# Attention with two mixtures of experts: weights converted from their upper 16 bits, engines chosen by the list, and the list's order kept on every compute engine in the first part

## The chip, the cores and the metric

The kernel runs on one core of one Trainium2 chip. The metric is the device time of one execution in microseconds (us). The kernel before has a median of 1095.64 us over 3 runs (1090.09 to 1098.15).

## The reference

Three blocks follow each other. Chunked attention works on q, k and v of 8 batches, 8 heads, 576 positions and 64 dimensions; every chunk of 64 positions attends to itself alone. Its output x has 4608 rows of 512. The second block is a feed-forward layer with a squared ReLU, and the third a soft mixture of 8 experts with 4 slots each:

```python
scores = scale * np.matmul(q_c, k_c.transpose(0, 1, 2, 4, 3))
attn = softmax(scores); out = np.matmul(attn, v_c)     # chunks of 64
h = np.maximum(x @ w_in, 0.0)                          # 512 -> 2048
x = h * h @ w_out                                      # 2048 -> 512
logits = x @ phi                                       # 32 slots
slot_input = softmax(logits, 0).T @ x
slot_out[e] = np.maximum(slot_input[e] @ w1[e], 0.0) @ w2[e]
out = softmax(logits, 1) @ slot_out
```

w_in and w_out lie in memory as 8-byte numbers (float64). [...]

## The kernel before, in words

The 4608 rows are cut into 36 tiles of 128, and the tiles into blocks: block 0 has one tile, block 1 two, blocks 2 to 12 three each. The hidden width 2048 is cut into 16 columns f of 128. A step (b, f) is the work of block b on column f. On TensorE (PE) it is `moe_h`, 12 matmuls (line 702), then, when the other engines have finished, `moe_out`, three matmuls per tile (lines 753, 754, 755). Between the two stand four elementwise instructions: relu (718 on ScalarE, ACT; 720 on VectorE, DVE), sq (725 or 727), gh (152, 157 or 161, the helper `copy`) and gl (737). gh and gl are the high and low part of the squared number, wi and wo the high and low parts of the weights.

A column of weights must be converted before its first step. `conv(f)` has two halves, a = 0 for w_in and a = 1 for w_out. `load` fetches 512 KB into a staging buffer, shifted by one byte, so that a number's top byte can be read as an int8 and 32 of the bits below it as an int32. `kept` (239 or 241, DVE) clips the top byte, `number` (246 ACT, 248 DVE or 250 GpSimd, POOL) copies it, `rest` (259 POOL, 254 DVE) subtracts the two, `lead` (line 154, ACT) scales the difference into the leading bits of a float, and `join` (265, DVE) shifts the int32 right by 5 and ors the leading bits in. Then `total`, `reduce` and `finish` (146, 169, 177 to 182) find a power-of-two scale of w_in, `hi` and `lo` (154 or 159, and 309) make wi, `whi` and `wlo` (152 or 157, and 319) make wo. There are four sets of staging buffers, and some sets are homes of later wo columns.

The attention of a tile i is a chain of its own. Tiles 0 to 6 run in 4-byte floats (`attention32`): transposes (576), copies to qbd and qkT, scores (593), max, less, exp, sums, normal (619), transposes (626), values (637), xh and xl (645, 650). Later tiles run in pairs of 2-byte parts (`attention`).

The first part of the program holds all 16 conversions, tiles 0 to 8 and the steps of blocks 0, 1, 2 and 13 (block 13 is a second pass over tiles 0 to 2 for the columns that blocks 0 and 1 left out). `list_schedule` orders it: each operation has a cost, an engine, what it depends on and a rank (`RANK_T`, `RANK_F`, `RANK_S`); the list takes, engine by engine, the operation that can start first, and among those that start within `AHEAD` (1.17 us) the one of lowest rank. The engine of an operation comes from tables written out by hand (`ON_U`, `ON_HI`, `ON_GL` and others). The phases of steps are set by `PARTS` = (7, 12): blocks 0 and 1 on f = 0 to 6, block 2 on f = 0 to 11, block 13 on f = 7 to 15, block 2 on f = 12 to 15. The list's order is binding on SyncE (SP), which issues the loads, alone (`IN_ORDER`); on the compute engines the framework's own scheduler places the instructions.

After the first part come blocks 3 to 12 with 16 steps each, in the order in which the code is written, and a tail with the experts.

Of the kernel before, what the change touches and what calls it, by code (L numbers as in the profile page):

```python
# [22 lines left out]
TOP = 2.0 ** 27  # L23
PARTS = (7, 12)
IN_ORDER = ('SP',)
AHEAD = 1.1702665353509787
ON_U = {(0, 0): 'act', (0, 1): 'act', (1, 0): 'act', (1, 1): 'pool', (2, 0): 'act', (2, 1): 'act', (3, 0): 'act', (3, 1): 'act', (4, 0): 'both', (4, 1): 'act', (5, 0): 'act', (5, 1): 'pool', (6, 0): 'act', (6, 1): 'act', (7, 0): 'act', (7, 1): 'act', (8, 0): 'dve', (8, 1): 'act', (9, 0): 'pool', (9, 1): 'act', (10, 0): 'act', (10, 1): 'pool', (11, 0): 'pool', (11, 1): 'pool', (12, 0): 'act', (12, 1): 'act', (13, 0): 'act', (13, 1): 'both', (14, 0): 'act', (14, 1): 'dve', (15, 0): 'act', (15, 1): 'dve'}
ON_PHI = {1: 1, 8: 1, 2: 1, 5: 1, 6: 0, 4: 1, 3: 1}
ON_WLO = {2: 0, 1: 1, 9: 0, 6: 1, 14: 1, 13: 0, 15: 0, 8: 1, 7: 1}
ON_SQ = {(0, 2): 'pool', (0, 1): 'pool', (0, 0): 'act', (13, 3): 'dve', (13, 2): 'dve', (2, 1): 'act', (2, 3): 'act', (1, 0): 'dve', (13, 0): 'pool', (0, 3): 'dve', (1, 2): 'dve'}  # L30
RANK_T = [-6.3129014593893205, 8.385327230567464, 13.762703571034038, 15.13222949110116, 41.022113092835795, 44.95494613298783, 56.80756465669842, 83.16639749144919, 93.32411425998357]
RANK_F = [-22.66145244618513, 22.55189538058041, 33.54199552023938, 45.42389033691279, 51.173403669572345, 53.0591736226747, 66.09437067068046, 77.9705914776398, 75.74661162051322, 94.18996216021172, 99.04476119923027, 98.70569850048518, 116.04666246008468, 115.83019197755651, 117.2519817658151, 162.90219728291348]
RANK_S = 13.647708445823483
# [5 lines left out]
ON_Q = {(6, 2): 'dve', (8, 1): 'act', (8, 3): 'dve', (4, 0): 'dve', (7, 0): 'act', (3, 0): 'dve', (0, 1): 'act', (2, 2): 'act', (4, 1): 'dve', (1, 1): 'dve', (7, 2): 'act', (1, 2): 'act', (4, 2): 'act', (4, 3): 'act', (3, 3): 'act', (0, 0): 'dve', (1, 0): 'dve', (6, 3): 'act', (6, 1): 'act'}  # L39
ON_V = {(5, 0): 'act', (2, 0): 'pool', (1, 1): 'dve', (7, 1): 'pool', (0, 1): 'act', (2, 1): 'pool', (6, 1): 'act', (3, 0): 'dve', (1, 0): 'act', (8, 1): 'act', (8, 0): 'dve'}  # L40
ON_N = {6: 'dve', 8: 'dve', 5: 'pool', 3: 'pool', 7: 'dve', 1: 'pool', 0: 'pool'}
ON_HI = {6: 'dve', 7: 'dve', 10: 'act', 15: 'dve', 8: 'act', 13: 'pool'}
ON_LEAD = {}
ON_WHI = {5: 'act', 9: 'dve', 3: 'dve', 14: 'dve', 6: 'act', 11: 'dve', 2: 'act', 15: 'dve', 7: 'act'}
ON_RELU = {(13, 3): 'dve', (1, 3): 'dve', (13, 0): 'act', (13, 1): 'act', (0, 0): 'dve', (1, 2): 'act', (2, 3): 'act', (0, 3): 'dve', (13, 2): 'act'}
ON_GH = {(1, 2): 'pool', (13, 3): 'dve', (13, 1): 'pool', (0, 0): 'act', (13, 0): 'act', (2, 3): 'dve', (13, 2): 'pool', (1, 0): 'act', (0, 3): 'pool', (1, 3): 'pool', (2, 1): 'act'}
ON_GL = {(13, 3): 'dve', (13, 0): 'dve', (2, 1): 'dve', (1, 2): 'dve', (0, 2): 'dve', (0, 1): 'pool'}


class Op:  # L50


    def __init__(self, eng, cost, deps, stage, fn):
        self.eng, self.cost, self.deps, self.stage, self.fn = eng, cost, deps, stage, fn
# [3 lines left out]
def kernel(  # L58
# [46 lines left out]
    ones = const.tile([P, P], BF16, name="ones")  # L105
    phi_sb = const.tile([P, KT, NS], F32, name="phi_sb")
# [88 lines left out]
    def conv(f):  # L195
# [40 lines left out]
        def kept(a):  # L236
            on_u = ON_U.get((f, a), "act")
            if on_u == "both":
                dve.tensor_scalar(half(a, 1), byte(a), 56.0, None, ALU.max)
            else:  # L240
                dve.tensor_scalar(half(a, 1), byte(a), -56.0, 56.0, ALU.max, ALU.min)

        def number(a):
            on_u = ON_U.get((f, a), "act")
            if on_u == "act":
                act.activation(out=half(a, 0), in_=byte(a), func=ACTF.Copy)  # L246
            elif on_u == "dve":
                dve.tensor_scalar(half(a, 0), byte(a), 1.0, None, ALU.mult)
            else:
                pool.tensor_scalar(half(a, 0), byte(a), 1.0, 1.0, ALU.mult, ALU.mult)  # L250

        def rest(a):
            if ON_U.get((f, a), "act") == "both":
                dve.scalar_tensor_tensor(
                    out=half(a, 1), in0=byte(a), scalar=-56.0, in1=half(a, 1),
                    op0=ALU.min, op1=ALU.add,
                )
# [1346 lines left out]
```

## Time and profile before

| | us |
|---|---|
| median of 3 runs (lowest, highest) | 1095.64 (1090.09, 1098.15) |
| the profiled execution, its own time | 1096.36 |
| its span, first to last instruction | 1094.6 |
| PE, DVE, ACT, POOL busy in it | 996.3, 638.1, 523.0, 253.2 |

The profile is one execution. "Busy" is the time in which an engine has an instruction under way; two instructions of one engine may overlap at their ends. [...] A wait is put down to the instruction whose end let the waiting one start. Line numbers are those of the kernel before.

### The profile page before, as it was taken

The page shows a single profiled execution, that of the slowest core. Times are in us where ns is not written, and L with a number is a line of the kernel's source. Part 1 is how long each engine was busy: PE and PEld are TensorE (multiplying, and loading weights), DVE is VectorE, ACT ScalarE, POOL GpSimd, SP SyncE. Part 2 cuts the span into 40 slices and gives each one's busy share as a digit, 9 for nine tenths or more (in the row PEclk, how much of TensorE's full clock was granted, in tenths as well). Part 3 has the DMA queues.
Part 4 walks back from the last instruction along what each step waited for, and adds up shares of the span by engine and source line. Part 5 has one row for each costly group of instructions (what it writes and reads, how often), then busy time and mean ns, then how long its engine had stood idle before and what let it go on. Part 6 is the DMA issues. An engine that isn't in the chain of part 4 may idle for free. (4 is left out here: it accounts for less than half of the span.)

```text
span 1094.6 us, 18390 instructions
## 1 busy us (share of the span) xinstructions
PE 996.3 (91%) x7144; PEld 680.7 (62%) x7144; DVE 638.1 (58%) x1318; ACT 523.0 (48%) x966; POOL 253.2 (23%) x255
## 2 busy tenths in 40 slices
PE   4574789888999999999999999999999999999993
PEld 3453556555666676667667676666666666666352
DVE  6887986777756655656656556566565462212232
ACT  4554556522645445455555455554454544434132
POOL 3544742422311111222111111221111121000100
PEclk8666789998999999999999999999999999999895
DMA  9452544114442222223333222243442342367998
GB/s 211 104 162 44 164 89 126 39 44 63 87 88 59 59 58 59 58 59 78 69 79 67 59 58 59 58 64 69 74 85 59 78 116 87 97 202 256 293 281 237
DMA packets 248471, 112.16 MB, mean 102 GB/s; under 512 B 208064, under 2 KB 241856, under 8 KB 248384
## 3 DMA queue, kind: packets, MB, share of 16 engines
q1 hardware_dynamic: 248384, 110.98, 42.1%
q8 instruction: 56, 0.92, 0.4%
q14 instruction: 31, 0.25, 0.1%
HBM read 78.71 MB, written 9.44 MB: 81 GB/s over the span
## 5 line engine op out<-in xcount | busy, mean ns | idle before, releaser
L702 PE MATMUL hps<-xb,wi 128*128 128x384 f16 (+2 forms) x2388 | 418.6, 326 | 15.1 <-ACT g L718 6.3
L702 PEld LDWEIGHTS <-wi 128*128 128x128 f16 x2388 | 219.0, 100 | 172.5 <-issue 49.5
L753 PE MATMUL x<-wo,gh 128*128 128x512 f32 x576 | 253.9, 441 | 19.4 <-ACT gh L152 10.2
L754 PE MATMUL x<-wo,gh 128*128 128x512 f32 x576 | 229.6, 399 | 0.0
L718 ACT ACTIVATE g<-hps,inv_w 128x384 f32<-128x384 f32 (+2 forms) x191 | 108.8, 570 | 233.6 <-PE hps L702 178.0
L755 PE MATMUL x<-wo,gl 128*128 128x512 f32 x576 | 214.7, 406 | 5.7 <-DVE gl L737 5.6
L737 DVE TENSOR_TENSOR gl<-g,gh 128x384 fp32r<-128x384 f32 (+2 forms) x196 | 112.6, 578 | 103.7 <-ACT gh L152 99.7
L753 PEld LDWEIGHTS x<-wo,gh 128*128 128x128 f32 x576 | 110.1, 191 | 58.8 <-ACT gh L152 12.1
L453 POOL TENSOR_TENSOR ex<-ex,rs 128x512 f32<-128x512 f32 x29 | 30.9, 1065 | 492.6 <-DVE rs L450 473.5
L755 PEld LDWEIGHTS x<-wo,gl 128*128 128x128 f32 x576 | 107.8, 191 | 35.4 <-DVE gl L737 12.2
L754 PEld LDWEIGHTS x<-wo,gh 128*128 128x128 f32 x576 | 110.4, 192 | 17.5 <-issue 0.8
L152 ACT ACTIVATE gh<-g 128x384 fp32r<-128x384 f32 (+2 forms) x186 | 94.9, 511 | 17.5 <-PE x L754 11.3
L725 ACT ACTIVATE g<-g 128x384 f32<-128x384 f32 (+2 forms) x184 | 95.1, 517 | 4.7 <-DVE g L720 0.2
L146 DVE TENSOR_REDUCE am<-qkv 128x1 bf16<-128x512 f32 x94 | 63.4, 684 | 42.4 <-DMA qkv<-in_k_dram 27.1
L407 DVE SCALAR_TENSOR_TENSOR vbd<-qkv,as,vbd 64x512 f16<-64x512 f32 x58 | 61.2, 1055 | 16.9 <-POOL vbd L402 16.3
L402 POOL TENSOR_SCALAR vbd<-qkv,as 64x512 f16<-64x512 f32 x58 | 57.5, 991 | 37.0 <-issue 31.6
L417 DVE COPY qbd<-qkT 64x1024 f16<-64x1024 f16 x58 | 25.5, 440 | 64.5 <-DMA qkT<-qk 64.1
L259 POOL TENSOR_TENSOR stage<-stage 128x512 bf16<-128x512 bf16 x30 | 46.2, 1584 | 63.6 <-ACT stage L246 60.2
L392 DVE SCALAR_TENSOR_TENSOR qk<-qkv,as,qk 128x512 f16<-128x512 f32 x58 | 55.1, 963 | 5.7 <-ACT qk L387 5.1
L486 ACT ACTIVATE xb<-misc 128x512 f16<-128x512 f32 x29 | 17.3, 597 | 65.6 <-PE misc L483 65.6
L387 ACT ACTIVATE qk<-qkv,as 128x512 f16<-128x512 f32 x58 | 38.6, 713 | 16.2 <-DVE as L179 15.8
L491 DVE SCALAR_TENSOR_TENSOR xb<-misc,xb 128x512 f16<-128x512 f32 x29 | 20.0, 690 | 39.4 <-ACT xb L486 39.4
(199 smaller groups left out, 1227.7 us busy)
## 6 DMA issues: line engine op xcount, KB each, us to landing
unit<-in_moe_w_dram SPq DMA_DIRECT2D x37, 512.0 KB, 4.3
unit<-in_moe_w_dram SPq DMA_DIRECT2D x54, 256.0 KB, 5.9
qkv<-in_q_dram SPq DMA_DIRECT2D x72, 128.0 KB, 3.4
qkv<-in_k_dram SPq DMA_DIRECT2D x72, 128.0 KB, 3.4
qkv<-in_v_dram SPq DMA_DIRECT2D x72, 128.0 KB, 3.2
stage<-in_moe_w_in_dram SPq DMA_DIRECT2D x16, 512.0 KB, 4.8
stage<-in_moe_w_out_dram SPq DMA_DIRECT2D x16, 512.0 KB, 5.7
out_dram<-o SPq DMA_DIRECT2D x16, 256.0 KB, 4.3
```

The costliest lines, as they stand in the source:

```text
L146: dve.tensor_reduce(out=am, in_=src, axis=AX.X, op=ALU.max, apply_absolute_value=True)
L152: act.activation(out=out, in_=in_, func=ACTF.Copy)
L392: dve.scalar_tensor_tensor(out=qk16[:, 2 * a + 1], in0=flat[:, a], scalar=v["s"][:, a : a + 1], in1=qk16[:, 2 * a], op0=ALU.mult, op1=ALU. ...
L402: pool.tensor_scalar(out=dst[0], in0=vin, scalar1=v["s"][pr, 2:3], scalar2=1.0, op0=ALU.mult, op1=ALU.mult,)
L407: dve.scalar_tensor_tensor(out=dst[1], in0=vin, scalar=v["s"][pr, 2:3], in1=dst[0], op0=ALU.mult, op1=ALU.subtract,)
L702: pe.matmul(hp, wi[f][:, wl, kt], xb[:, xl, kt, :n], start=(nm == 0), stop=(nm == 3 * KT - 1))
L718: act.activation(out=r["g"], in_=r["hp"], func=ACTF.Relu, scale=inv_w[f])
L725: act.activation(out=g, in_=g, func=ACTF.Square)
L737: (dve if ON_GL.get((b, f // 4), "dve") == "dve" else pool).tensor_tensor(out=r["gl"], in0=r["g"], in1=r["gh"].bitcast(F32), op=ALU.subtract)
L753: pe.matmul(o, gh[:, c], wo[f][:, 0], start=first, stop=False)
L754: pe.matmul(o, gh[:, c], wo[f][:, 1], start=False, stop=False)
L755: pe.matmul(o, gl[:, c], wo[f][:, 0], start=False, stop=last)
```

## The change

The conversion reads the upper 16 bits. `load` shifts by two bytes instead of one, and the top 16 bits of each 8-byte number are then an int16. `upper` (new) multiplies it by 2^19 into a 4-byte float, on ACT, DVE or POOL; `join` is now three DVE instructions: clip from below, clip from above and add as an integer, and the shift (by 13) and or. `kept`, `number`, `rest` and `lead` are gone. The float goes to a part of the first qk16 buffer, the integer to a part of the first p16 buffer, one place each for all columns; so the `upper` of a column waits for the `join` of the same half one column before, and tile 8, which uses qk16, for the last of them.

The list chooses engines. The tables are gone: an operation may name several engines with a cost for each, and an engine takes it unless another would end it earlier by more than a margin (`SLACK`). Costs are new, ranks too, `AHEAD` is 0.01 us, and `PARTS` is (8, 11): blocks 0 and 1 on f = 0 to 7, block 2 on f = 0 to 10, block 13 on f = 8 to 15, block 2 on f = 11 to 15. The list goes on until tiles 0 to 8 are done. `IN_ORDER` names SP and all four compute engines.

```diff
-PARTS = (7, 12)
-IN_ORDER = ('SP',)
-AHEAD = 1.1702665353509787
-ON_U = {...}
...
+PARTS = (8, 11)
+IN_ORDER = ("SP", "PE", "DVE", "Activation", "Pool")
+AHEAD = 0.01
+HOP = 0.15
+SLACK = {'act': 3.5, 'dve': -2.69, 'pool': -0.65}
+LEAST = 18432.0
...
-                out=raws[a].bitcast(I8)[:, 1 : 1 + 4096].rearrange("p (k f) -> p k f", k=4),
+                out=raws[a].bitcast(I8)[:, 2 : 2 + 4096].rearrange("p (k f) -> p k f", k=4),
...
+        def upper(a, eng):
+            h = raws[a].bitcast(I16)[:, 4 : 4 + 2048].rearrange("p (n t) -> p n t", t=4)[:, :, 0]
+            v[a] = qk16_b[(N32 + 1) % 2].rearrange("p a n -> p (a n)").bitcast(F32)[
+                :, 512 * a : 512 * a + 512
+            ]
+            if eng == "act":
+                act.activation(out=v[a], in_=h, func=ACTF.Relu, scale=2.0 ** 19, bias=least)
             else:
+                (dve if eng == "dve" else pool).tensor_scalar(
+                    v[a], h, -LEAST, 2.0 ** 19, ALU.max, ALU.mult
                 )
+            v["off", a] = LEAST if eng == "act" else 0.0
         def join(a):
+            m = p16_b[(N32 + 1) % 2].rearrange("p a n -> p (a n)").bitcast(F32)
+            s, off = 2.0 ** 19, v["off", a]
+            dve.tensor_scalar(m, v[a], (14336.0 + off) * s, -2 * off * s, ALU.max, ALU.add)
             dve.scalar_tensor_tensor(
-                out=word(a), in0=word(a), scalar=5, in1=top(a),
+                out=m.bitcast(I32), in0=v[a], scalar=(off - 14336.0) * s, in1=m,
+                op0=ALU.min, op1=ALU.add,
+            )
+            dve.scalar_tensor_tensor(
+                out=word(a), in0=word(a), scalar=13, in1=m.bitcast(I32),
                 op0=ALU.logical_shift_right, op1=ALU.bitwise_or,
             )
...
+                    at_ = max(r, free[e])
+                    if len(op.on) > 1 and min(
+                        max(r, free[x]) + c for x, c in op.on.items() if x != e
+                    ) + SLACK.get(e, 0.0) < at_ + op.on[e]:
+                        continue
```

On DVE before, among the first conversions after column 0, the clips (241) and the joins (265) of several halves stand apart, with attention between them (qkv, ex and xb are a tile's, stage a column's).

```order
L241 TENSOR_SCALAR stage<-stage 128x512
L600 TENSOR_REDUCE mx<-misc 128x8
L241 TENSOR_SCALAR stage<-stage 128x512
L603 TENSOR_TENSOR ex_75<-misc,mx 128x512
L241 TENSOR_SCALAR stage<-stage 128x512
L265 SCALAR_TENSOR_TENSOR stage<-stage 128x512
L177 TENSOR_SCALAR a32g<-misc 128x1
L614 TENSOR_REDUCE su<-ex_75 128x8
L146 TENSOR_REDUCE wam<-stage 128x1
L178 TENSOR_SCALAR a32g<-a32g 128x1
L241 TENSOR_SCALAR stage<-stage 128x512
L615 TENSOR_SCALAR su<-su 128x8
```

With the change a half is three instructions in a row (262, 263, 267), and the copies to qbd that stood on DVE before are not among them.

```order
L596 TENSOR_TENSOR ex_75<-misc,mx 128x512
L162 TENSOR_REDUCE wam<-stage 128x1
L593 TENSOR_REDUCE mx<-misc 128x8
L607 TENSOR_REDUCE su<-ex_75 128x8
L608 TENSOR_SCALAR su<-su 128x8
L609 RECIPROCAL rs<-su 128x8
L596 TENSOR_TENSOR ex_76<-misc,mx 128x512
L262 TENSOR_SCALAR p_77<-qk_73 128x512
L263 SCALAR_TENSOR_TENSOR p_77<-qk_73,p_77 128x512
L267 SCALAR_TENSOR_TENSOR stage<-stage,p_77 128x512
```

Five instructions per half on three engines have become four on two, and on DVE they follow each other. On POOL before, in the stretch of block 2 and block 13, the conversion's subtraction (259) stands between the low parts of wo (319).

```order
L453 TENSOR_TENSOR ex_75<-ex_75,rs 128x512
L468 TENSOR_TENSOR p_77<-ex_75,p_77 128x512
L259 TENSOR_TENSOR stage<-stage 128x512 x2
L319 TENSOR_TENSOR wo_1875<-stage,wo_1875 128x512
L259 TENSOR_TENSOR stage<-stage 128x512
L161 TENSOR_SCALAR wi_2053<-stage,ws 128x512
L319 TENSOR_TENSOR wo_1963<-stage,wo_1963 128x512
L161 TENSOR_SCALAR gh<-g 128x384 x3
L259 TENSOR_TENSOR stage<-stage 128x512 x2
L161 TENSOR_SCALAR gh<-g 128x384 x2
L259 TENSOR_TENSOR stage<-stage 128x512 x2
L319 TENSOR_TENSOR wo_2210<-stage,wo_2210 128x512
```

With the change the conversion is gone from POOL, and the low part gl of each step (723) stands there.

```order
L723 TENSOR_TENSOR gl<-g,gh 128x384
L313 TENSOR_TENSOR wo_1416<-stage,wo_1416 128x512
L755 TENSOR_TENSOR iv_1438<-a32i 128x1
L723 TENSOR_TENSOR gl<-g,gh 128x384
L755 TENSOR_TENSOR iv_1486<-a32i 128x1
L755 TENSOR_TENSOR iv_1489<-a32i 128x1
L313 TENSOR_TENSOR wo_1484<-stage,wo_1484 128x512
L723 TENSOR_TENSOR gl<-g,gh 128x384
L313 TENSOR_TENSOR wo_1538<-stage,wo_1538 128x512
L723 TENSOR_TENSOR gl<-g,gh 128x384
L313 TENSOR_TENSOR wo_1595<-stage,wo_1595 128x512
L723 TENSOR_TENSOR gl<-g,gh 128x384 x2
```

In the first part 38 gl stand on POOL with the change, 3 before; all 32 `upper` stand on ACT.

## Rows read from the trace of the kernel before

**Rows 1.** The page, busy tenths in 40 slices of the span.

```profile
PE   4574789888999999999999999999999999999993
PEclk8666789998999999999999999999999999999895
```

**Rows 2.** Stages: us, PE, PEld, DVE, ACT, POOL busy (instructions), PEclk, DMA share, GB/s.

```profile
0.00:34.40 34.40, 13.72 (x158) 11.48 (x159) 23.85 (x48) 16.22 (x21) 15.20 (x24) 0.84 0.94 203
34.40:151.20 116.80, 77.31 (x628) 55.34 (x626) 99.02 (x191) 59.54 (x103) 59.76 (x54) 0.71 0.45 113
151.20:200.50 49.30, 48.08 (x272) 32.54 (x271) 33.18 (x74) 32.54 (x55) 15.97 (x12) 1.00 0.31 91
200.50:252.50 52.00, 45.39 (x299) 30.50 (x298) 38.87 (x80) 16.86 (x27) 16.32 (x16) 0.97 0.14 46
252.50:267.70 15.20, 11.89 (x56) 8.96 (x55) 10.60 (x18) 1.50 (x3) 4.47 (x5) 0.78 0.75 105
280.00:1004.00 724.00, 722.02 (x5078) 497.84 (x5077) 395.35 (x832) 363.23 (x695) 128.62 (x131) 1.00 0.36 80
```

**Rows 3.** The same stages, out matmuls of line 753 alone.

```profile
34.40:151.20 116.80, 10.61 (x21) 4.60 (x21) 0.71 0.45 113
151.20:200.50 49.30, 15.71 (x37) 6.86 (x37) 1.00 0.31 91
200.50:252.50 52.00, 12.03 (x28) 5.20 (x27) 0.97 0.14 46
252.50:267.70 15.20, 6.28 (x13) 3.03 (x12) 0.78 0.75 105
```

**Rows 4.** Waits from 0 to 160 us: us, times, longest.

```profile
POOL stage L259 <- ACT stage L246: 29.4, 10, 5.9
PE misc L626 <- POOL ex L619: 13.7, 3, 8.8
PE x L753 <- ACT gh L152: 10.2, 6, 4.5
DVE stage L241 <- DMA stage<-in_moe_w_in_dram: 6.9, 7, 1.4
```

**Rows 5.** Groups by form, 0 to 200 us: count | busy us, mean ns | idle before.

```profile
L259 POOL TENSOR_TENSOR stage<-stage 128x512 bf16<-128x512 bf16 x26 | 40.0, 1573 | 48.9 <-ACT stage L246 45.4 <-DVE stage L248 3.2
L265 DVE SCALAR_TENSOR_TENSOR stage<-stage 128x512 int32<-128x512 int32 x28 | 25.9, 928 | 10.0 <-ACT stage L154 9.8
L246 ACT ACTIVATE stage<-stage 128x512 bf16<-128x512 int8 x19 | 25.8, 1369 | 17.8 <-DVE stage L241 17.2 <-DVE rs L616 0.4 <-DVE a32i L182 0.2
L241 DVE TENSOR_SCALAR stage<-stage 128x512 bf16<-128x512 int8 x26 | 24.8, 956 | 10.3 <-DMA stage<-in_moe_w_in_dram 8.6 <-DMA stage<-in_moe_w_out_dram 1.7
L154 ACT ACTIVATE stage<-stage 128x512 int32<-128x512 bf16 x28 | 19.0, 682 | 9.0 <-POOL stage L259 5.4 <-DVE stage L254 3.5
L309 DVE SCALAR_TENSOR_TENSOR wi<-stage,ws,wi 128x512 f16<-128x512 f32 x12 | 9.2, 784 | 1.3 <-ACT wi L154 1.2
L619 POOL TENSOR_TENSOR ex<-ex,rs 128x512 f32<-128x512 f32 x6 | 7.0, 1160 | 10.0 <-DVE rs L616 10.0
L650 DVE SCALAR_TENSOR_TENSOR xb<-misc,a32s,xb 128x512 f16<-128x512 f32 x6 | 6.3, 1048 | 0.0
L737 POOL TENSOR_TENSOR gl<-g,gh 128x128 fp32r<-128x128 f32 x3 | 1.8, 607 | 2.5 <-ACT gh L152 2.5
L157 DVE CAST wo<-stage 128x512 fp32r<-128x512 f32 x3 | 1.3, 420 | 0.0
```

**Rows 6.** Lines 241 and 146, all instructions: min/median/max ns, first and last start.

```profile
L241 DVE TENSOR_SCALAR stage<-stage x30: 694/752/1915, 4.7 to 229.8; 128x512 bf16<-128x512 int8 x30
...
L146 DVE TENSOR_REDUCE am<-qkv x94: 667/689/692, 12.1 to 848.0; 128x1 bf16<-128x512 f32 x94
```

**Rows 7.** DVE in order of time: start us, duration us.

```profile
70.07 0.75 DVE L650 SCALAR_TENSOR_TENSOR xb<-misc,a32s,xb 128x512 f16<-128x512 f32 x1
70.73 0.14 DVE L179 TENSOR_SCALAR ws<-wg 128x1 int32<-128x1 int32 x1
```

More of the change, by code (lines that the diff above doesn't have):

```diff
@@ L38, with __call__, cost_of, only @@
 N32 = 7
[L39 to L47, printed above, removed]
 class Op:
     def __init__(self, eng, cost, deps, stage, fn):
-        self.eng, self.cost, self.deps, self.stage, self.fn = eng, cost, deps, stage, fn
+        self.on = dict(eng) if isinstance(eng, dict) else {eng: cost}
+        self.eng = next(iter(self.on))
+        self.choose = isinstance(eng, dict)
+        self.deps, self.stage, self.fn = deps, stage, fn
+    def __call__(self):
+        self.fn(self.eng) if self.choose else self.fn()
+def cost_of(kind, n):
+    return {
+        "read": {"act": 0.23 + 0.00088 * n, "dve": 0.08 + 0.00105 * n},
+        "scaled": {"act": 0.26 + 0.00092 * n, "dve": 0.08 + 0.00105 * n},
+        "copy": {"act": 0.2 + 0.00083 * n, "dve": 0.1 + 0.0007 * n, "pool": 0.2 + 0.0011 * n},
+        "two": {"dve": 0.07 + 0.00105 * n, "pool": 0.2 + 0.0021 * n},
+        "square": {
+            "act": 0.2 + 0.00083 * n, "dve": 0.07 + 0.00105 * n, "pool": 0.2 + 0.0021 * n,
+        },
+    }[kind]
+def only(costs, *engines):
+    return {e: costs[e] for e in engines}
 @with_exitstack
@@ L105 @@
     ones = const.tile([P, P], BF16, name="ones")
+    two = const.tile([P, 2], F32, name="two")
+    one, least = two[:1, 0:1], two[:, 1:2]
     phi_sb = const.tile([P, KT, NS], F32, name="phi_sb")
@@ L243, in number @@
[L243 to L256, printed above, removed]
-                )
-            else:
-                pool.tensor_tensor(out=half(a, 1), in0=half(a, 0), in1=half(a, 1), op=ALU.subtract)
@@ L669, in attention32 @@
-        ops["max"] = Op("dve", 0.6, ["qk"], 3, largest)
-        ops["less"] = Op("dve", 0.6, ["max", *old("Tp")], 3, less)
-        ops["exp"] = Op("act", 0.52, ["less"], 3, exp)
-        ops["sums"] = Op("dve", 0.8, ["exp"], 4, sums)
-        ops["normal"] = Op(on_n, {"dve": 0.6, "pool": 0.95}[on_n], ["sums"], 4, normal)
+        ops["kc"] = Op(cost_of("read", 512), None, ["T1", *old("qk")], 1, kcopy)
+        ops["qk"] = Op("pe", 1.9, ["qd0", "qd1", "kc"], 2, scores)
+        ops["max"] = Op("dve", 0.61, ["qk"], 3, largest)
@@ L674, in attention32 @@
+        ops["less"] = Op("dve", 0.61, ["max", *old("Tp")], 3, less)
+        ops["exp"] = Op("act", 0.63, ["less"], 3, exp)
+        ops["sums"] = Op("dve", 0.85, ["exp"], 4, sums)
+        ops["normal"] = Op({"pool": 1.16, "dve": 0.61}, None, ["sums"], 4, normal)
         ops["Tp"] = Op("pe", 0.5, ["normal"], 5, ptrans)
-        on = ON_Q.get((i, 3), "act")
-        ops["pc"] = Op(on, {"dve": 0.6, "act": 0.48}[on], ["Tp", *old("pv")], 6, pcopy)
+        ops["pc"] = Op(cost_of("read", 512), None, ["Tp", *old("pv")], 6, pcopy)
@@ L1246, in list_schedule @@
         left_s = 0
[L1247 removed]
+        while ph < len(left) or left_s or any(avail.values()):
             best = None
```

241 lines of the change are left out of this document (98 added, 143 removed).

## The prediction, made before the change was run

> **What bounds the kernel now.** I read the page's row of slices first, to see where PE is not full. It is at 9 tenths in nearly every slice from the eleventh on, and at 4 to 8 before; the granted clock is low in the same early slices [rows 1]. One slice is 27 us, so the loss lies in the first 270 us, the first part of the program. Next I cut the span into stages. From 280 to 1004 us PE is busy 722.0 of 724 us at full clock [rows 2]: that stretch is PE's own work, is not in the diff, and I carry it over unchanged, as I do the tail. What can change is when it begins.
>
> The out matmuls of line 753 count the steps, since each tile's step has one. There are 21 up to 151.2 us, then 37, 28 and 13 to 267.7 us; a matmul that lies across a boundary is counted on both sides, three do, and what is left is the first part's 96 [rows 3]. So blocks 0 and 1 end their seven columns at 151 us, and the first part ends at 267.6 us. Its two halves have different limits. From 34.4 us, where the first tile's `xl` stands, to 151.2 us DVE is busy 99.0 of 116.8 us (85%), PE 77.3 us at a clock of 0.71, ACT and POOL about half [rows 2]. From 151.2 to 267.7 us PE is busy 105.4 of 116.5 us (48.1, 45.4 and 11.9) [rows 2].
>
> The waits say what DVE's load does. POOL's subtraction waits 29.4 us for ACT's copy of the byte, and PE waits 13.7 us for POOL's normal (619) and 10.2 us for gh [rows 4]. These are chains through three engines, each late by a little. Idle time of DVE is small, so the first half is held by DVE's work and by hand-overs around it.
>
> **The change part by part.** A half of a conversion costs, before, on DVE 0.96 (241) and 0.93 us (265), on ACT 1.37 (246) and 0.68 us (154), on POOL 1.57 us (259) [rows 5]. With the change `upper` is on ACT in all 32 cases. Its nearest row is line 154, also a strided 2-byte read on ACT: 0.68 us; the other end is 1.37 us, the int8 read. I take 0.68. ACT so loses 1.37 us per half, POOL 1.57.
>
> On DVE the three joins are not in the trace. The shift-and-or is the old one, 0.93 us. The add of the two clips reads two tensors like `lo` (309), 0.78 us, with bounds 0.75 and 0.93. The first clip is a one-input instruction: 0.42 us by line 157, 0.96 by line 241 [rows 5]; I take 0.6. That is 2.31 us against 1.88: DVE pays 0.43 us more per half, 14 us in 32 halves. If this were all, the first half would get longer.
>
> What pays for it is what leaves DVE. The order has DVE's rows up to `lo` of f = 7, the last column that phase one needs. From the first `xl` on they are 13 halves (30.0 us at 2.31), 8 `lo` (6.3 at 0.784), 16 reductions (11.0 at 0.69 [rows 6]), the max, subtraction, sum and `xl` of 5 tiles (15.6, three at 0.69 and `xl` at 1.05 [rows 5]), and 67 small ones (10.1 at 0.15): 73.0 us. Not among them are qbd and qkT copies, relu, sq, gh and gl, which ACT and POOL now do. Instructions on DVE begin before the one ahead ends: `xl` begins at 70.07 us and lasts 0.75, and the next is at 70.73 [rows 7]. That is 0.085 us for each of some 150, 12.7 us, and leaves 60.3 us.
>
> At DVE's share of before, 0.85, this takes 71 us. I start it at 34.4 us as before, though two tiles of loads now go ahead of the first weights. `lo` of f = 7 is then at 105.5 us. The remaining steps take some 6.5 us: a step of three tiles is 4.1 us of PE (49.3 us for twelve [rows 2, 3]), and one elementwise chain of 2.4 lies between. Phase one ends at 112 us, with 8 columns instead of 7.
>
> What is left is 72 tile steps instead of 75. Before, 75 took 116.5 us with the attention of tiles 6 to 8 and 11 us of waits. Less one step of 4.1 us that is 112.4 us, and I keep the waits. The first part ends at 112 + 112.4 = 224.4 us.
>
> Is a conversion late for that? From `lo` of f = 7 to that of f = 15 DVE has 17 halves (39.3 us), 8 `lo` (6.3), 14 reductions (9.7), 37 small ones (5.6) and 5.4 us of tile 7 and of stores: 66.3, less 10 of overlap, 56.3 us; at 0.85, 66 us. f = 15 is ready at 172 us. PE wants it after 18 more steps, at 112 + 74 = 186 us. PE is the later one by 14 us: in the second half PE stays the bound.
>
> ACT takes the copies, but is given back 32 times 1.37 us. POOL loses 32 times 1.57 us, 50 us, and gets 35 more gl. A gl of 384 columns on POOL is not in the trace; 0.61 us for 128 columns and 1.16 for a two-input 512 bound it [rows 5], and I take 1.0, some 30 us in all. A step's chain of four grows by some 0.4 us, and in the order two or more steps of PE lie between a step's h and its out, which hides it. If that cover is gone, 24 steps of 0.4 us are 10 us.
>
> The sum is made on the profiled execution, 1096.36 us. 267.6 less 224.4 is 43.2 us, and 1096.36 − 43.2 = 1053.2 us. The profiled execution stands 0.7 us above the median; I round to 1053.
>
> One behaviour weighs against the change. Line 241, whose median is 0.75 us, took up to 1.92 us; the reductions of line 146 never left 0.67 to 0.69 us [rows 6]. Some kinds of DVE instruction are held by something and others not. [...] My 2.31 us holds a mean hold of 0.2 us each already; the rest of it is the second rival.
>
> **The rivals.** Better: DVE is fuller, since its three joins need no other engine between them. At a share of 0.92 `lo` of f = 7 is at 34.4 + 65.5 = 100 us, phase one ends at 106.4, and with PE's busy time alone (105.4 − 4.1 = 101.3 us) the part ends at 207.7 us: 1036 us. For it: POOL's wait of 29.4 us goes. Against it: the clock of 0.71 in that stretch, which makes PE's 77 us of work long.
>
> Held by POOL: POOL's instructions are 1.0 to 1.4 us long, and a join or a `lo` that meets one waits half of it, 0.52 us, instead of the 0.2 us that I counted. 112 such (96 joins, 16 `lo`) add 36 us: 60.3 + 56.3 + 36 = 152.6 us, at 0.85 180 us, f = 15 at 214 us. After it come PE's last 38.4 us (224.4 − 186), so the part ends at 253 us: 1082 us. For it: the maxima of rows 6. Against it: POOL has less to do than before.
>
> Slower, by blocked queues: with the list's order binding everywhere, a DVE instruction that waits (a first clip for its `upper` on ACT, a max for PE's scores) holds all that stands behind it, ready or not, and PE and ACT then wait for DVE. This shows as DVE's share. The part ends at 72.8 + 116.6 / share once DVE paces it, below 0.77; at 0.60 it ends at 267.6 us, where it ends now. At 0.55 it is 284.8 us: 1114 us. For it: 32 hand-overs from ACT to DVE, and costs in the list that the chip need not keep. Against it: DVE's share of 0.85 before was reached in an order fixed ahead, too.
>
> The change does not do what it says: the loads pace the conversions. The first three stages moved 24.7 MB in 200.5 us (their GB/s by their length), 123 GB/s, and all four to 252.5 us 27.1 MB. At that rate 27.1 MB need 220 us, f = 15 is late, and the part ends near 263 us: 1092 us. For it: line 241 waited 6.9 us for loads [rows 4]. Against it: the same queue moved 203 GB/s in the first 34.4 us, and its share was 0.45 and 0.31 after [rows 2].
>
> **How the numbers follow.** The forecast, 1053 us with an own range of 1040 to 1068 (DVE's share down to 0.70 gives 239 us and 1068), has 0.50; the better case 0.17, held by POOL 0.15, blocked queues 0.12, loads 0.06. A measurement of this kernel can tell about 1% (11 us) from no change. Faster by more are the first two and most of the third: 0.79. Within 1% are the loads and a little of the third: 0.09. Slower is 0.12. The range leaves out half of the better case below 1026 us and the slower one with some of the loads above 1090 us.
>
> **What would show it.** Right: the 96th out matmul of line 753's successor near 224 us; its 24th near 112 us; the last `lo` near 172 us; DVE's share near 0.85 up to there; the first clip at 0.6 us, the add near 0.78, `upper` near 0.68; PE full and at full clock from 112 us on; the stretch behind the first part as long as before. Wrong: the first clip above 1 us in the mean (held by POOL); DVE idle before 262 for ACT, with its share under 0.7 (blocked queues); DVE waiting for loads by tens of us; or a stretch behind the first part that is longer than 827 us (1094.6 − 267.6), which I exclude since PE fills it.

## The result and the profile after

The changed kernel takes 1043.45 us (median of 4 runs, 1038.68 to 1045.08). The kernel before took 1093.62 us in the same comparison (4 runs). The ratio is 0.9532 with a 95% interval of 0.9482 to 0.9582: faster by 4.7%. The forecast was 1053 us, faster. All stretches below are of one profiled execution each: 1038.68 us with a span of 1036.7 us after, against 1096.36 and 1094.6 us before. The one after is the fastest of its four runs, so the stretches below differ by 57.9 us in all, while the medians lie 50.2 us apart.

The page after, the slices that answer to [rows 1], and the line of busy times. PEclk is the clock that TensorE was granted, as a share of its full clock (in the slices in tenths):

```profile
PE   5777998999999999999999999999999999999983
PEclk9889999999999999999999999999999999999895
PE 974.1 (94%) x7156; PEld 671.1 (65%) x7156; DVE 606.8 (59%) x1257; ACT 524.7 (51%) x997; POOL 237.2 (23%) x260
```

PE is full from the fifth slice on (but for one at 8 tenths) instead of the eleventh, and the low clocks of the early slices are gone (8, 6, 6 and 6 tenths in the first four before, 9, 8, 8 and 9 now). PE's busy time fell from 996.3 to 974.1 us, though its work is the same.

The first part of the program as one stretch, before and then after, and the step to the 97th out matmul (columns as in [rows 2]):

```profile
0.00:267.60 267.60, 196.28 (x1400) 138.72 (x1401) 205.52 (x408) 126.66 (x205) 111.72 (x109) 0.83 0.44 107
267.60:280.00 12.40, 11.41 (x98) 7.64 (x96) 8.91 (x19) 7.33 (x15) 3.53 (x5) 1.00 0.19 43
```

```profile
0.00:215.70 215.70, 176.92 (x1418) 129.77 (x1419) 168.10 (x335) 127.63 (x235) 95.16 (x111) 0.96 0.50 127
215.70:224.10 8.40, 8.40 (x53) 5.03 (x52) 6.94 (x15) 5.34 (x10) 2.39 (x3) 1.00 0.23 53
```

The first part lost 51.9 us. PE's idle time in it went from 71.3 to 38.8 us, which is 32.5; PE's busy time for nearly the same count of matmuls went from 196.3 to 176.9 us, which is 19.4, at a mean clock of 0.96 instead of 0.83. So on PE's row nearly two fifths of the gain are shorter matmuls. This splits the time; it does not say that the clock caused that share. The out matmuls of phase one, against the first row of [rows 3]:

```profile
23.10:110.70 87.60, 10.54 (x24) 4.84 (x24) 0.90 0.67 178
```

One of them takes 0.44 us in the mean, 0.51 before. DVE's 205.5 us became 168.1, POOL's 111.7 became 95.2. The rest of the span is 821.0 us instead of 827.0.

The stages after, cut at the first `xl`, the 24th out matmul, the 57th, the 84th, the 96th and the 97th:

```profile
23.10:110.70 87.60, 66.28 (x677) 51.78 (x678) 77.61 (x163) 55.84 (x109) 42.45 (x47) 0.90 0.67 178
110.70:160.70 50.00, 45.94 (x238) 30.81 (x237) 46.24 (x86) 32.52 (x59) 24.10 (x23) 1.00 0.36 99
160.70:203.80 43.10, 41.30 (x284) 28.80 (x283) 29.44 (x50) 22.05 (x40) 18.00 (x21) 1.00 0.26 62
203.80:215.70 11.90, 11.90 (x97) 9.17 (x96) 2.50 (x7) 5.37 (x10) 5.72 (x6) 1.00 0.12 24
224.10:949.00 724.90, 723.64 (x5115) 500.26 (x5114) 403.81 (x850) 366.05 (x701) 130.27 (x135) 1.00 0.37 81
```

DVE is busy 77.6 of 87.6 us in phase one (89%). After it DVE and PE are both at 92% for 50 us, and only then does DVE ease. The out matmuls (line 739, the successor of 753) stand at 38.2 us (the first), 110.7 (24th), 160.7 (57th), 203.8 (84th), 215.7 (96th) and 224.1 us (97th).

PE's waits after (us, times, longest), first from 23.1 to 110.7 us, then from 110.7 to 204 us:

```profile
PE misc L185 <- DVE wam L162: 6.4, 5, 1.9
PE hps L688 <- DVE wi L303: 3.9, 4, 2.7
PE misc L619 <- POOL ex L612: 3.3, 3, 1.9
...
PE misc L185 <- DVE wam L162: 5.2, 3, 2.7
PE x L741 <- POOL gl L723: 0.3, 1, 0.3
```

Of the two waits of [rows 4] the one for POOL's normal (13.7 us) is 3.3 us now, and the one for gh (10.2 us) is gone. The longest was 2.7 us before (line 169, up to 152 us): the matmul that reduces a column's largest value over the partitions (185) stands at a fixed place in PE's order, and PE waits there for DVE.

### The profile page after: what moved, and what is told of

Read it like the earlier page. It is cut to its first block, busy times and chain, and to the rows that moved or that the text cites. A ratio compares the mean times of both kernels' runs of the same rounds, so it can differ in the third digit from the quotient of the medians.

```text
span 1036.7 us, 18460 instructions
## 1 busy us (share of the span) xinstructions
PE 974.1 (94%) x7156; PEld 671.1 (65%) x7156; DVE 606.8 (59%) x1257; ACT 524.7 (51%) x997; POOL 237.2 (23%) x260
## 4 chain that ended last, share of the span: by engine, by line
PE 78%; DVE 9%; DMA 5%; SPq 2%; ACT 2%; issue 2%; POOL 0%; DVEq 0%; ACTq 0%; POOLq 0%
PE hps L688 32%; PE x L739 12%; PE x L741 11%; PE x L740 11%; DVE p L263 2%; DVE stage L267 2%; DMA stage<-in_moe_w_in_dram 2%; DMA out_dram<-o 2%; PE ehps L1437 2%; PE misc L865 1%; DVE p L262 1%; PE misc L878 1%; PE misc L948 1%; SPq L1508 1%; PE sop L1523 1%
## 5 line engine op out<-in xcount | busy, mean ns | idle before, releaser
L688 PE MATMUL hps<-xb,wi 128*128 128x384 f16 (+2 forms) x2400 | 413.4, 322 | 4.1 <-DVE wi L303 3.9
L739 PE MATMUL x<-wo,gh 128*128 128x512 f32 x576 | 249.9, 434 | 0.8 <-DVE x2sb L766 0.6
L740 PE MATMUL x<-wo,gh 128*128 128x512 f32 x576 | 227.4, 395 | 0.0
L741 PE MATMUL x<-wo,gl 128*128 128x512 f32 x576 | 217.0, 400 | 2.0 <-POOL gl L723 2.0
L704 ACT ACTIVATE g<-hps,inv_w 128x384 f32<-128x384 f32 (+1 forms) x198 | 111.3, 562 | 210.1 <-PE hps L688 174.2
L723 DVE TENSOR_TENSOR gl<-g,gh 128x384 fp32r<-128x384 f32 x162 | 92.1, 572 | 95.7 <-ACT gh L168 94.6
L739 PEld LDWEIGHTS x<-wo,gh 128*128 128x128 f32 x576 | 108.8, 189 | 39.1 <-ACT g L711 5.9
L740 PEld LDWEIGHTS x<-wo,gh 128*128 128x128 f32 x576 | 108.9, 189 | 17.1 <-POOL wo L313 0.2
L168 ACT ACTIVATE gh<-g 128x384 fp32r<-128x384 f32 (+2 forms) x196 | 100.2, 512 | 19.0 <-PE x L740 14.5
L711 ACT ACTIVATE g<-g 128x384 f32<-128x384 f32 (+1 forms) x196 | 100.3, 512 | 4.8
L395 POOL TENSOR_SCALAR vbd<-qkv,as 64x512 f16<-64x512 f32 x58 | 53.8, 928 | 44.0 <-issue 13.1
L723 POOL TENSOR_TENSOR gl<-g,gh 128x384 fp32r<-128x384 f32 (+2 forms) x38 | 36.6, 966 | 35.4 <-ACT gh L168 29.4
```

Source lines behind the costliest of these rows:

```text
L168: act.activation(out=out, in_=in_, func=ACTF.Copy)
L395: pool.tensor_scalar(out=dst[0], in0=vin, scalar1=v["s"][pr, 2:3], scalar2=1.0, op0=ALU.mult, op1=ALU.mult,)
L688: pe.matmul(hp, wi[f][:, wl, kt], xb[:, xl, kt, :n], start=(nm == 0), stop=(nm == 3 * KT - 1))
L704: act.activation(out=r["g"], in_=r["hp"], func=ACTF.Relu, scale=inv_w[f])
L711: act.activation(out=g, in_=g, func=ACTF.Square)
L723: (dve if eng == "dve" else pool).tensor_tensor(out=r["gl"], in0=r["g"], in1=r["gh"].bitcast(F32), op=ALU.subtract)
```

## The experiments

Ratios are against runs of the kernel before on the same chip; the changed kernel's 0.953 is the other end. A difference of two ratios is given in us by 1096.

**The old conversion in the new list, and the list's order on SyncE alone.** The first puts the five old instructions of a half into the changed kernel, with the copy of the byte on ACT in all halves; list, engine choice, ranks and binding order stay.

```diff
-            ops[f"up{a}"] = Op({"act": 0.72, "dve": 0.65, "pool": 1.5}, ...)
-            ops[f"join{a}"] = Op("dve", 1.65, [f"up{a}"], ...)
+            ops[f"kept{a}"] = Op("dve", 0.7, [f"load{a}"], ...)
+            ops[f"num{a}"] = Op({"act": 1.37}, None, [f"kept{a}"], ...)
+            ops[f"rest{a}"] = Op("pool", 1.5, [f"num{a}"], ...)
+            ops[f"lead{a}"] = Op("act", 0.69, [f"rest{a}"], ...)
+            ops[f"join{a}"] = Op("dve", 0.65, [f"lead{a}"], ...)
```

> The changed kernel with the old conversion from the top byte put back (clip on DVE, copy on ACT in all 32 halves, subtraction on POOL, scaling on ACT, join on DVE); list, engine choice and binding order stay. Theory A (the short conversion is worth much, because it frees POOL and ACT and has fewer hand-overs): POOL gets back 15 x 1.5 us and ACT 15 x 1.4 us in a phase one of 88 us in which they were busy 42 and 56 us, and the chain of a half is five steps again; 15 to 30 us longer than the changed kernel, 1058 to 1073 us. Theory B (the gain is the list's engine choice and its order; the conversion costs DVE about as much either way): within 8 us of the changed kernel's 1043 us.

Measured: 1070.29 us, ratio 0.9776 (0.9735 to 0.9818). The old conversion costs 27 us inside the new list, as the first theory expected. Its 24th out matmul is at 141.7 us instead of 110.7:

```profile
30.00:141.70 111.70, 73.72 (x606) 55.35 (x604) 93.36 (x180) 81.93 (x137) 75.32 (x70) 0.72 0.65 156
```

DVE is busy 84% of that stretch (89% in the changed kernel's phase one), but ACT and POOL carry 82 and 75 us instead of 56 and 42, PE's clock is 0.72, and the phase ends 31 us later. The list, told of other costs, also made another order: 11 `lo` begin before the 24th out matmul instead of 8. How much of the 27 us is that order was not tried.

```diff
-IN_ORDER = ("SP", "PE", "DVE", "Activation", "Pool")
+IN_ORDER = ("SP",)
```

> The changed kernel with the list's order binding on SyncE alone; the framework's scheduler places the instructions of the four compute engines, as it did before. Engines and conversion stay as changed. Theory A (work moved off DVE is the gain): within 8 us of 1043 us. Theory B (the order kept on every engine is a good part of the gain): 1055 to 1080 us, the loss in phase one, where PE would wait again for gh, normal and the reductions of the weights.

Measured: 1052.84 us, 0.9618 (0.9576 to 0.966). Without the binding order the changed kernel loses 9 us. This lies between the two cases expected, and the two intervals still overlap by a little, so its size is uncertain. The 96th out matmul is at 222.4 us.

**Each half of the change alone, and both in the old list.** Three versions of the kernel before: with the new conversion, with the binding order, and with both. The tables, ranks and phases are those of before.

```diff
+            ops[f"up{a}"] = Op("act", 0.72, [f"load{a}", *last], ...)
+            ops[f"join{a}"] = Op("dve", 1.65, [f"up{a}"], ...)
```

> The kernel before with the new conversion alone (upper on ACT in all halves, three joins on DVE), with its own list, tables and order. Theory A (short conversion): the five-step chain and POOL's 29 us of waiting go, 10 to 25 us faster than before: 1069 to 1084 us. Theory B (DVE is the bound and pays 0.4 us more per half, 14 us in all): the same as before or up to 14 us slower, 1090 to 1108 us.

```diff
-IN_ORDER = ('SP',)
+IN_ORDER = ("SP", "PE", "DVE", "Activation", "Pool")
```

> The kernel before with the list's order binding on all compute engines, nothing else changed. Theory B (a binding order is good in itself): 1060 to 1085 us. Theory A (an order made with costs that do not fit the chip, as in this list, where DVE's first clip counts 0.34 us and takes 0.96, blocks the queues): 1095 to 1140 us.

> The kernel before with the new conversion (all upper on ACT) and with the list's order binding on every compute engine; old tables, PARTS (7, 12), AHEAD 1.17. It fills in the fourth corner: neither 1.000, new conversion alone 0.987, binding order alone 1.025. If the two parts simply add, 1.025 x 0.987 = 1.012, about 1106 to 1112 us. If the binding order lost its time only to the old conversion's hand-overs (five instructions on three engines, each a place where a bound queue can stand), it should now be near the new conversion alone, 1075 to 1085 us, or below it by the 9 us that the binding brought in the changed kernel's list. If the loss is that of a list whose end is not filled (tiles 7 and 8 come behind the last steps), the 96th out matmul may be early, near 250 us, and the gap to the 97th stays at 30 us or more.

Measured: the conversion alone 1080.23 us, 0.9873 (0.9831 to 0.9915); the order alone 1123.04 us, 1.0254 (1.0203 to 1.0305); both 1122.78 us, 1.0261 (1.0232 to 1.0289). They do not add: the conversion is worth 14 us where the framework's scheduler places the instructions, and nothing where the old list binds. The binding costs 42 us on top of the new conversion. Two views of the version with both say where. First the stretch from its 96th out matmul (269.6 us) to its 97th (306.0 us):

```profile
269.60:306.00 36.40, 13.43 (x127) 9.67 (x125) 23.48 (x48) 9.10 (x17) 8.61 (x11) 0.62 0.45 94
```

Then PE's waits up to 310 us:

```profile
PE misc L459 <- DMA pT<-p: 16.0, 1, 16.0
PE misc L172 <- DVE wam L149: 15.9, 6, 3.9
...
PE misc L406 <- DVE qbd L395: 7.0, 1, 7.0
```

The old list ends before the attention of tile 8: its last instructions for that tile make the high parts of q, k and v. In the bound order PE stands through the rest of that chain, before the scores (406) and before the values (459): 36.4 us with 13.4 us of work, where the unbound version needs 12.6 us (252.7 to 265.3). The other 17 us are lost before (96th out at 269.6 instead of 252.7 us). So the first two expectations for the version with both fall, and the third holds in part: the gap is there, but the 96th out matmul is late as well. The changed kernel's list goes on to the end of tile 8, and there the gap is 8.4 us. Of these two lists, the binding order is a gain only with the one made for it.

From before to after in one chain: the conversion 14 us, the new list with its choice of engines 28 us (0.9873 to 0.9618), the binding 9 us. Which part of the new list brings the 28 us (costs, choice, ranks, phases, its later end) was not tried.

**The low part of the squared number on DVE alone.**

```diff
-            "gl": Op(cost_of("two", P * n), None, ["gh"], 0, lambda e: moe_gl(b, f, e)),
+            "gl": Op(only(cost_of("two", P * n), "dve"), None, ["gh"], 0, lambda e: moe_gl(b, f, e)),
```

> The changed kernel with the low part gl of every step on DVE alone (35 gl of the first part go from POOL back to DVE). Theory A (work that left DVE is part of the gain): DVE gets 22 x 0.55, 8 x 0.43 and 8 x 0.28 us, 18 us in all less four it has already; in phase one some 5 us at a share of 0.89, in the second half the rest, where DVE was busy 46 of 50 us: 1048 to 1060 us. Theory B (POOL's instructions hold DVE's joins, and gl on POOL costs more in held joins, 0.6 us a half, than it saves): 1030 to 1041 us, the mean of the first clip falling from 0.66 towards 0.45 us.

Measured: 1067.61 us, 0.9752 (0.9732 to 0.9772), 24 us slower than the changed kernel: worse than any case expected. The joins did get shorter, as the theory of the holds by POOL says. Its rows (min/median/max ns):

```profile
L262 DVE TENSOR_SCALAR p<-qk x32: 375/419/1534, 18.1 to 200.7; 128x512 f32<-128x512 f32 x32
L263 DVE SCALAR_TENSOR_TENSOR p<-qk,p x32: 680/693/1682, 18.5 to 201.1; 128x512 int32<-128x512 f32 x32
L267 DVE SCALAR_TENSOR_TENSOR stage<-stage,p x32: 681/693/770, 19.3 to 201.9; 128x512 int32<-128x512 int32 x32
```

By the means of the three lines a half costs 0.36 us less (0.58, 0.80 and 0.70 us), 11 us in 32 halves. Against that stand 40 gl on DVE, 22.6 us (24 of 384 columns at 0.67 us in the mean, 16 smaller ones at 0.41), where the changed kernel has two, 1.1 us. That is 10 us more work for DVE on balance. The phase up to the 24th out matmul became 13.5 us longer (124.2 us), at the same share of DVE:

```profile
23.10:124.20 101.10, 68.71 (x690) 53.37 (x691) 89.83 (x208) 65.55 (x125) 31.86 (x31) 0.86 0.59 160
124.20:165.90 41.70, 41.04 (x211) 28.57 (x210) 21.07 (x42) 20.49 (x39) 8.95 (x13) 1.00 0.14 48
```

DVE did 12.2 us more in phase one; at 0.89 that is 13.7 us, the whole delay. But only 7.5 us of it are gl. The list, left with one engine for gl, made another order, and 20 halves and 10 `lo` stand on DVE in this phase instead of 16 and 8:

```profile
L262 DVE TENSOR_SCALAR p<-qk 128x512 f32<-128x512 f32 x20 | 11.4, 569 | 3.6 <-ACT qk L250 3.5
```

In the next 42 us DVE was half idle. How much of the 24 us is gl and how much this order was not tried. What the run does show is DVE's own balance: taking gl off POOL shortened its joins by 11 us and gave it 21.5 us of gl.

**Longer joins, early or late.** The first clip is done three times instead of once, writing the same numbers, for the columns below 8 in one run and from 8 on in the other. The list is not told.

```diff
-            dve.tensor_scalar(m, v[a], (14336.0 + off) * s, -2 * off * s, ALU.max, ALU.add)
+            for _ in range(3 if f < 8 else 1):
+                dve.tensor_scalar(m, v[a], (14336.0 + off) * s, -2 * off * s, ALU.max, ALU.add)
```

> The changed kernel with the first clip of a join done three times instead of once for f = 0 to 7 (same result), so 16 halves have two more DVE instructions of 0.45 to 0.66 us: 14 to 21 us of DVE work. The list's costs are not told of it. Theory A (DVE's work sets phase one): 14 to 24 us longer, 1057 to 1067 us, with the 24th out that much later. Theory B (phase one is held by PE or by waits between engines, and DVE has room): less than 7 us, under 1050 us.

> The changed kernel with the first clip of a join done three times for f = 8 to 15, so the same 14 to 21 us of DVE work, after phase one. Theory A (PE sets the second half, with f = 15 ready at 180 us some 5 to 10 us before PE wants it): 3 to 12 us longer, 1046 to 1055 us. Theory B (DVE sets the second half as well): 14 to 24 us longer, as in the early case.

Measured: early 1058.98 us, 0.9671 (0.9653 to 0.9689); late 1058.61 us, 0.9669 (0.9652 to 0.9687). Both lose 15 us against the changed kernel. In the early one the phase up to the 24th out matmul has these busy times:

```profile
23.10:126.40 103.30, 73.28 (x677) 57.23 (x678) 90.39 (x194) 56.39 (x110) 40.17 (x47) 0.80 0.57 151
```

DVE's share is 0.88, as without the repeats; 12.8 us more of its work made the phase 15.7 us longer, so DVE sets phase one. The late one decides the point on which the prediction had fixed itself, that PE has 14 us in hand in the second half. It has not. The rows that show it cut the second half at the last `wi` (line 303, 304 where the clip is repeated). It begins at 180.1 us in the changed kernel and at 198.0 us in the late run, and ends some 1.3 us after. First the changed kernel, then the late run, from the 24th to the 96th out matmul:

```profile
110.70:181.40 70.70, 64.84 (x335) 44.10 (x334) 59.40 (x109) 45.43 (x82) 34.25 (x36) 1.00 0.30 85
181.40:215.70 34.30, 34.30 (x284) 24.68 (x283) 18.78 (x32) 14.51 (x27) 13.56 (x14) 1.00 0.28 55
```

```profile
L304 DVE SCALAR_TENSOR_TENSOR wi<-stage,ws,wi x16: 624/752/1485, 26.2 to 198.0; 128x512 f16<-128x512 f32 x16
...
112.30:199.50 87.20, 71.71 (x343) 46.28 (x342) 72.91 (x138) 45.84 (x82) 33.15 (x36) 0.94 0.23 64
199.50:232.40 32.90, 32.90 (x277) 23.97 (x275) 19.15 (x32) 14.30 (x27) 13.36 (x14) 1.00 0.27 57
```

Up to the last `wi` DVE's share is 0.84 in both (59.4 of 70.7, 72.9 of 87.2), so 13.5 us more work are 16.5 us more time; behind it PE is full for 33 to 34 us in both. So in these two the first part ends a nearly fixed stretch of PE after the last column is converted, and DVE sets when that is.

The fixed stretch alone would not show this. In all ten kernels with the new list, the changed one among them, the 96th out matmul came 28.8 to 34.4 us after the end of the last `wi`, wherever that was between 181 and 214 us. The run with the old conversion is one of them (31.1 us), and there PE is full and DVE half idle from the 24th to the 96th out matmul:

```profile
141.70:244.90 103.20, 98.78 (x602) 68.62 (x602) 49.62 (x85) 62.47 (x106) 51.08 (x50) 0.98 0.18 49
```

With 28.6 us less work of DVE than in the changed kernel (78.2 us) this stretch is 103.2 instead of 105.0 us. More work of DVE costs its full time there; less, in this one run, gave next to nothing back.

**Was it the list's wrong costs?** PE's waits for wam rose to 15.0 us in the late run, so the delay could have come from an order made with joins that are too cheap. Two runs tell the list: one gives every join a cost of 2.1 instead of 1.65, near what it takes on the chip; the other repeats the late run with a cost of 2.85 for the columns from 8 on.

```diff
-            ops[f"join{a}"] = Op("dve", 1.65, [f"up{a}"], 1 + a, lambda a=a: join(a))
+            ops[f"join{a}"] = Op("dve", 2.1, [f"up{a}"], 1 + a, lambda a=a: join(a))
```

> The changed kernel with one number of the list changed: a join costs 2.1 us instead of 1.65 (the three instructions took 0.66, 0.92 and 0.85 us in the mean, about 2.2 less overlaps). Ranks and margins stay. Theory A (a binding order is worth what its costs fit the chip): PE's 12 us of waiting for the weights' reductions shrink, 1030 to 1041 us. Theory B (the ranks were chosen with the cost of 1.65, and another order made from them is worse): 1046 to 1060 us. Within 3 us of 1043: neither matters.

```diff
-            ops[f"join{a}"] = Op("dve", 1.65, [f"up{a}"], 1 + a, lambda a=a: join(a))
+            ops[f"join{a}"] = Op("dve", 2.85 if f >= 8 else 1.65, [f"up{a}"], 1 + a, lambda a=a: join(a))
```

> The changed kernel with the first clip done three times for the columns from 8 on, as in the run before that did so and took 1058.6 us, but with the list told: the cost of a join in the list is 2.85 instead of 1.65 for those columns. Theory W (the loss of the second half came from an order made with wrong costs: PE's queue stood for the reduction matmul): PE's waits for wam fall from 15 us to 5 or less and the time comes back to 1043 to 1050 us. Theory D (DVE's work itself is what the second half waits for): the time stays at 1055 to 1062 us and PE waits elsewhere, for wi or for gh.

Measured: 2.1 gives 1044.66 us, 0.9544 (0.9527 to 0.9562), no change; the late joins told give 1064.78 us, 0.9736 (0.9705 to 0.9768), 6 us worse than untold. PE's waits up to 300 us, in the first of the two:

```profile
PE hps L688 <- DVE wi L303: 5.9, 6, 1.9
...
PE hps L688 <- ACT g L704: 4.2, 3, 2.1
...
PE misc L185 <- DVE wam L162: 3.1, 6, 0.8
```

The wait for wam fell from 11.6 us (the changed kernel, up to 226 us) to 3.1, as it should, and others took its place (for wi 5.9 us instead of 3.9, for g 4.2 instead of 0.3): the last `wi` ended at 187.5 us instead of 181.4, the 96th out matmul came at 218.3 instead of 215.7 us. In the late run told, the wait for wam fell only to 12.5 us, and the last `wi` ended at 206.2 us. The theory of the wrong costs falls with the first of the two: the wait for wam names where PE stands when DVE is late, not the cause. The second adds that the list, told of the joins, did not win the time back.

**How much is the one order worth?** `AHEAD` 0.1 and 0.3 instead of 0.01, which moves a few instructions.

```diff
-AHEAD = 0.01
+AHEAD = 0.1
```

> The changed kernel with AHEAD 0.1 instead of 0.01: of the operations that can start within 0.1 us the list takes the one of lowest rank, so a few stand elsewhere. If the list's small choices are worth little, 1040 to 1050 us; if the changed kernel's order is a single lucky one among many, 1050 to 1065 us. Under 1038 us it would be a better version than both.

> As the run before, with AHEAD 0.3. If the list's small choices are worth little, 1040 to 1050 us; if the changed kernel's order is a single lucky one among many, 1050 to 1070 us.

Measured: 1049.38 us, 0.959 (0.956 to 0.9621), and 1050.13 us, 0.9599 (0.957 to 0.9629). The first lies just inside the case of small choices and the second on the border of the two cases, some 6 us above the changed kernel. The intervals overlap with its own, so that the changed order is better than its neighbours, by half a per cent, is likely but not shown. None of the versions beat the changed kernel.

## Why the prediction was right, and the step that failed

The forecast stands 0.9% above the median. By its own terms, in the profiled execution:

| term | predicted | measured | difference |
|---|---|---|---|
| first `xl` begins | 34.4 | 23.1 | −11.3 |
| from there to the eighth `lo` | 71 | 75.4 | +4.4 |
| from there to the 24th out matmul | 6.5 | 12.2 | +5.7 |
| 24th to 96th out matmul | 112.4 | 105.0 | −7.4 |
| end of the first part to the end of the span | 827 | 821 | −6.0 |

The differences add to −14.6 us, and 1053.2 − 14.6 is 1038.6 us, the execution's own time.

**The start.** It was taken over from before. The first `xl` began between 21 and 26 us in all kernels with the new list, the one with the old conversion among them (22.7 us), so the list is enough for it. In the old list the new conversion alone (28.1 us) and the binding alone (26.8 us) brought it forward too. Two terms behind it were too small and hid most of it: phase one ended at 110.7 us against 112.

**DVE's work in phase one.** The instructions of DVE from 23.1 to 98.5 us, grouped by form, and the stretch itself:

```profile
L263 DVE SCALAR_TENSOR_TENSOR p<-qk,p 128x512 int32<-128x512 f32 x13 | 12.0, 920 | 0.4
L267 DVE SCALAR_TENSOR_TENSOR stage<-stage,p 128x512 int32<-128x512 int32 x13 | 11.9, 916 | 0.4
L262 DVE TENSOR_SCALAR p<-qk 128x512 f32<-128x512 f32 x13 | 10.4, 799 | 0.5 <-ACT qk L250 0.4
L303 DVE SCALAR_TENSOR_TENSOR wi<-stage,ws,wi 128x512 f16<-128x512 f32 x8 | 5.7, 727 | 1.7 <-ACT wi L170 1.7
...
23.10:98.50 75.40, 54.08 (x601) 43.11 (x602) 69.82 (x153) 47.39 (x89) 37.12 (x40) 0.90 0.64 175
```

The counts were right: 13 halves, 8 `lo`. The halves took 34.3 us, not 30.0. All groups add to 77.2 us, not 73.0, and the overlaps took off 7.4 us, not 12.7. So DVE was busy 69.8 us instead of 60.3, and its share was 0.93, not 0.85, as the better rival had it. Two errors of opposite sign left 4.4 us. Over all 32 halves the three joins had means of 0.66, 0.92 and 0.85 us, 2.43 against 2.31. `upper` took 0.76 us, near the row that 0.68 was taken from and far from the other bound, 1.37. A gl of 384 on POOL took 1.10 us against 1.0:

```profile
L250 ACT ACTIVATE qk<-stage,two 128x512 f32<-128x512 int16 x32 | 24.4, 764 | 5.3 <-DMA stage<-in_moe_w_in_dram 2.3 <-DVE p L263 1.4 <-issue 1.2
L723 POOL TENSOR_TENSOR gl<-g,gh 128x384 fp32r<-128x384 f32 x22 | 24.2, 1103 | 23.6 <-ACT gh L168 18.3 <-issue 4.9 <-POOL gl L723 0.4
```

**The step that failed** is "PE is the later one by 14 us: in the second half PE stays the bound". The last column was to be ready at 172 us and PE to want it at 186. It was ready at 181.4 us. PE from there:

```profile
181.72 6.02 PE L688 MATMUL hps<-xb,wi 128*128 128x384 f16 x36
```

By the program's order these are three steps of 12 matmuls, and the second, from 183.7 us, is the first that needs the last column. So 2 us were in hand, not 14. The late run shows what that means, since work on DVE there costs its full time. The size came out all the same because PE lost little by it. From the 24th to the 96th out matmul PE is idle 5.9 us (64.8 and 34.3 busy of 105.0), nearly all of it in the waits for wam (5.2 us), where the prediction had carried over 11 us from before; and it is busy 99.1 us instead of 101.3. That is the −7.4 us. DVE and PE are balanced there: less work of DVE could give PE back 5.9 us at most, and the run with the old conversion got 1.8 of them; more work costs its full time. The 10 us named as the price of a longer chain over gl were not paid: PE waited 0.3 us for POOL's gl in that stretch.

**The stretch behind the first part**, which was carried over unchanged, became 6 us shorter: 4.0 us up to the 97th out matmul (8.4 us, full, instead of 12.4) and 2.0 us after it. Of the 4.0 us, 3.0 are work of PE that no longer stands there (53 matmuls instead of 98).

**The rivals.** Better: its 1036 us are nearer to the profiled execution (1038.7) than the forecast's 1053.2; from the median the two are 7 and 10 us away. Two of its own terms were measured, DVE's share (0.93 against 0.92) and a second half in which PE is hardly idle. It shares the forecast's start and DVE's work, the one 11.3 us too late and the other 9.5 us too small, and these nearly cancel. So that either number came out is in part luck. Held by POOL: the holds are there, 0.51 us in the mean, about the 0.52 that this rival took, but in 39 of the 96 joins and 3 of the 16 `lo`, not in all; they cost 0.6 us a half, the size that was counted. Taking gl from POOL removed more than half of them and gained nothing, though in another order, so this mechanism is real and did not decide. Blocked queues: not in this kernel, where the binding gains some 9 us, but it is just what happened in the old list, at +42 us with the new conversion, by the place where that list ends and not only by DVE's share. Loads: `upper` on ACT waited 2.3 us for w_in in the first part and DVE 4.8 us for v, far from the tens of us that this rival needs.

## What to carry to other kernels

Before a list's order is bound on all engines, see whether the list reaches past the point where the next work can start: the same switch was worth −9 us with a list that did and +42 us with one that ended before. Where one engine prepares what another consumes, a busy consumer does not show that it has time in hand: here DVE's share was 0.84 and PE's 0.92, and more work on DVE still cost its full time. Add work to the preparing engine and take some away, and see by how much the end moves each time. A wait that names one matmul says where a queue stands, so before it is removed by another order, lengthen the work that it waits for and see whether the whole moves: here the wait for wam fell from 11.6 to 3.1 us by another order, and the time stayed (1044.66 against 1043.45 us).

## What the runs showed of the hardware that was not expected

How exactly POOL holds DVE. DVE first, then POOL, in order of time (start us, duration us):

```profile
60.08 1.41 DVE L263 SCALAR_TENSOR_TENSOR p<-qk,p 128x512 int32<-128x512 f32 x1
...
66.66 0.68 DVE L162 TENSOR_REDUCE wam<-stage 128x1 bf16<-128x512 f32 x1
67.25 2.08 DVE L262 TENSOR_SCALAR p<-qk 128x512 f32<-128x512 f32 x1
```

```profile
59.90 1.04 POOL L612 TENSOR_TENSOR ex<-ex,rs 128x512 f32<-128x512 f32 x1 [3.80 <-PE x L741]
...
67.25 1.80 POOL L147 MEMSET qbd<- 128x2048 f16 x1
```

The add (263) ends at 61.49 us, 0.55 us after POOL's instruction (60.94). The clip (262), which meets the memset, takes 2.08 us and ends at 69.33 us, 0.28 us after it (69.05); its median without gl on POOL is 0.42 us. Of the 96 joins 39 were held, that is, took over 0.06 us more than the medians of their lines without gl on POOL (0.42, 0.69 and 0.69 us): 20.0 us in all, 0.6 us a half. Every held clip ended 0.28 to 0.29 us and every held add or shift 0.54 to 0.55 us after the end of a POOL instruction: by these ends they did not run slower but stood until POOL was done. Three of the 16 `lo` (303) did the same: they took 1.00, 1.25 and 1.50 us against a median of 0.75, and ended 0.54 to 0.55 us after a POOL instruction. The clip at 59.67 us, which began 0.23 us before POOL's instruction of 59.90, took 0.37 us and was not held. No reduction of line 162 was held: 20 in the first part stood beside a POOL instruction, and all took 0.67 to 0.69 us. The memset that held the clip reads no tile (`qbd<-`). What lets POOL hold the one kind and not the other, no trace here shows.

The other surprise is PE's clock, with which two fifths of the first part's gain stand on PE's row as shorter matmuls: in phase one the mean granted clock was 0.71 before [rows 2] and 0.90 after, 0.72 with the old conversion in the new list and 0.80 with longer early joins. As DVE sets that phase, no run shows whether the higher clock made it shorter or came with it.
